# Attention with a gated MLP on one core: where the partial products of the query projection are read, in which order VectorE folds, and when two token quarters are gated

## The chip, the cores and the metric

The kernel runs on one core of one Trainium2 chip. The metric is the device time of one execution in microseconds (us); the number given for a kernel is the median of its runs. A core has several engines with queues of their own: TensorE (PE: matmuls, and PEld: the loading of their weights), VectorE (DVE), ScalarE (ACT), GpSimd (POOL) and SyncE (SP), whose queue issues nearly all DMAs here. Each engine works through its own instructions in order; between engines, semaphores tell when a result is there or a buffer is free. SBUF is the working memory, PSUM the small memory in eight banks that matmuls write into.

## The reference

Sizes: 2048 tokens of width 512, 32 heads of width 128, 2048 cached keys per head, an MLP of width 1792. Inputs are bf16.

```python
xn = layernorm(x)
q = (xn @ wq) split into 32 heads
p = softmax(q @ k_cache.T * 128 ** -0.5)         # per head
s = concat(p @ v_cache) @ wo                     # attention
x1 = xn + shifted(gelu(layernorm(xn) @ w1)) @ w2 # the mixer
g = silu(x1 + gelu(layernorm(x1) @ w3) @ w4)
out = x + s * g
```

## The kernel before, in words

**Head of the program** (about 118 us): layer norms, the mixer and most of the MLP branch, whose result g (up to a factor 0.5) stays in `xall`, one tile of 128 tokens by 512 per token tile t (0 to 15). The rest of the MLP is spread over the first units.

**Units and slots.** The attention is 128 units: `units` lists group g (8 groups of 4 heads), token quarter qt (4 quarters of 512 tokens), head hh in the group, in this order of nesting. A unit has eight slots (`SPU`), n counts slots over all units, u is the unit and p the slot in it. The long loop (L903 on) writes out by hand, slot by slot, in which order every engine gets its instructions; `pin` keeps that order. A slot on TensorE is: two score matmuls (`s_slot`, L405, into one of two PSUM buffers `ps_s`), two value matmuls of ten slots ago (`pv_slot`, L437), then, in some slots, query products and one matmul of the output projection (`wo_mm`, L500; the list `at_wo` gives the slots). ScalarE takes the exponential of the slot's scores, 128x1024 from PSUM to `pT` (L416).

**What VectorE does per unit.** It sums the exponentials over the key blocks, four blocks of 512 at a time: `add_first` (L422, slot 4), `add_next` (L427, slot 6 and slot 0 of the next unit), then folds four blocks to two (`fold`, L431) and two to one (`fold_last`, L435), all in slot 0 of the next unit. In slot 3 SP issues the transposing DMA of that block (`turn`, L460). A unit later, in slot 0 too, `turned_sums` reduces the transposed block (L465), takes the reciprocal (L467) and sends it to DRAM; `bcast` (L473) brings it back, spread over partitions, and `norm` (L485, slot 7) multiplies it into the unit's attention output. `wo_post` (L533) adds a tile's output projection to `sacc` (L549).

**Query projection in pairs.** From unit 14 to 123 the queries of two heads at a time (units v and v+1) come from seven products of half blocks instead of eight (`product`, L363; sums of x and differences of wq are prepared in `x_sum` and `w_sum`, L361). A pair's products 1, 6, 2, 7, 5, 4, 3 are issued at slots 1, 2, 5, 8, 9, 12, 13 counted from the start of unit v-2. They go to one PSUM tile `ps_q` of two halves (256 columns each, together one bank): first M1 in half 0 and M6 in half 1, then M2 is added to half 0; a new tile takes M7 and M5, then M4 is added to half 0 and M3 to half 1. There is one such buffer (psX, tag "xa"), shared in the same order. `q_part` (L383) reads on VectorE what is needed in between:

- part 0, slot 3: a copy m1 = M1 (L388), u = M6 + m1 (L389)
- part 1, slot 6: first quarter of the queries, a copy of M1+M2 (L392)
- part 2, slot 11: u3 = M7 + u (L397), fourth quarter = M5 + u3 (L398)
- part 3, slot 14: the two middle quarters = both halves + u (L400)

So product 2 comes after part 0, product 7 after part 1, product 4 after part 2, and the next pair's product 1 after part 3.

**Gating and output.** For most tiles, in the last group (g = 7) `wo_post` adds the projection to `sacc` (L549), multiplies by the gate (L558), adds x (L560) and sends the tile out (L561). For quarters in `LATE` (before: the last one, tiles 12 to 15) the gate goes in early: after group `GY - 1` (before: 6) `sacc` is multiplied by the gate (`y_scale`, L515) and x is added (`y_add`, L520), in later slots, one tile after the other; from group `GY` on the projection is gated by itself (L542, into `tm`), and either added to `sacc` (L545, if a group follows) or, in the last group, added to it on the way out (`y_out`, L524, when `pay` is called). The last unit and the last quarter's output are written out by hand from L970 on.

Of the kernel before, what the change touches and what calls it, by code (L numbers as in the profile page):

```python
# [8 lines left out]
ACT = mybir.ActivationFunctionType  # L9
ALU = mybir.AluOpType  # L10
FP32 = mybir.dt.float32
BF16 = mybir.dt.bfloat16
# [5 lines left out]
def kernel(  # L18
# [15 lines left out]
    nc = tc.nc  # L34
    P = nc.NUM_PARTITIONS
# [9 lines left out]
    QT = Sq // 512  # L45
# [6 lines left out]
    NG = H // HG  # L52
# [9 lines left out]
    pin = tc.keep_in_program_order  # L62
# [28 lines left out]
    qp2 = ent(pool("qp2", 2))  # L91
    smp = ent(pool("smp", 4))
# [18 lines left out]
    def mm(out, lhsT, rhs, start, stop, **kw):  # L111
# [9 lines left out]
        out=ident[:], in0=diag[:], scalar1=0.0, scalar2=None, op0=ALU.is_equal))  # L121
# [1 line left out]
    HEAD = 7  # L123
    XS = 3 * QT + 1
    units = [(g, qt, hh) for g in range(NG) for qt in range(QT) for hh in range(HG)]
    LATE = (QT - 1,)
    GY = NG - 1
    NU = len(units)
    TURN = range(NU - HG)
    NS = NU * SPU  # L130
    kTs, vBs, wqs, wos, oTs, st = {}, {}, {}, {}, {}, {}
# [202 lines left out]
    sw = {}  # L334
# [28 lines left out]
    def product(v, k):  # L363
# [16 lines left out]
        for dc in range(2):  # L380
            mm(s["ps"][:, side, :], b[:, dc, :], x[:, dc, :], k in (1, 7) and dc == 0, True, skip_group_check=True)

    def q_part(v, i):  # L383
        s = sw[v]
        ps, t = s["ps"], lambda: pS.tile([P, 256], FP32, tag="tq", bufs=3, name="tq")
        if i == 0:
            m1, s["u"] = t(), t()
            pin(nc.vector.tensor_copy(out=m1[:], in_=ps[:, 0, :]))  # L388
            pin(nc.vector.tensor_tensor(out=s["u"][:], in0=ps[:, 1, :], in1=m1[:], op=ALU.add))  # L389
        elif i == 1:  # L390
            q = s["q"] = qp2.tile([P, 4, 256], BF16, name="qT")
            pin(nc.vector.tensor_copy(out=q[:, 0, :], in_=ps[:, 0, :]))  # L392
            for j in range(2):
                st[v + j] = dict(qT=q[:, 2 * j:2 * j + 2, :].rearrange("d a b -> d (a b)"))
        elif i == 2:
            u3 = t()
            pin(nc.vector.tensor_tensor(out=u3[:], in0=ps[:, 0, :], in1=s["u"][:], op=ALU.add))  # L397
            pin(nc.vector.tensor_tensor(out=s["q"][:, 3, :], in0=ps[:, 1, :], in1=u3[:], op=ALU.add))  # L398
        else:
            pin(nc.vector.tensor_tensor(  # L400
                out=s["q"][:, 1:3, :], in0=ps[:], in1=s["u"][:].unsqueeze(1).to_broadcast([P, 2, 256]),
                op=ALU.add))
            del sw[v]
# [21 lines left out]
    def add_next(u, i):  # L425
        a = st[u]["acc"]
        pin(nc.vector.tensor_tensor(out=a[:], in0=a[:], in1=st[u]["pT"][i][:], op=ALU.add))  # L427
# [5 lines left out]
    def fold_last(u):  # L433
        a = st[u]["acc"]
        pin(nc.vector.tensor_tensor(out=a[:, 0, :], in0=a[:, 0, :], in1=a[:, 1, :], op=ALU.add))  # L435
# [25 lines left out]

    def turned_sums(u):
        s = st[u]
        sm = smp.tile([P, 4], FP32, name="sm")
        pin(nc.vector.tensor_reduce(out=sm[:], in_=s["tT"][:], axis=mybir.AxisListType.X, op=ALU.add))  # L465
        rc = smp.tile([P, 4], FP32, name="rc")
        pin(nc.vector.reciprocal(out=rc[:], in_=sm[:]))  # L467
        s["dr"] = drp.tile([P, 4], FP32, name="dr")
        pin(nc.sync.dma_start(out=s["dr"][:], in_=rc[:]))
# [190 lines left out]
    for jc in range(DC):  # L660
        b = BASE_J[jc]
# [200 lines left out]
    UA, UB = NU - 2, NU - 1  # L862
# [12 lines left out]
    pairs = range(FIRST, LAST + 1, 2)  # L875
    q_plan = defaultdict(list)
    steps = defaultdict(list)
    for v in pairs:
        a = (v - 2) * SPU
        for k, n in ((1, 1), (6, 2), (2, 5), (7, 8), (5, 9), (4, 12), (3, 13)):  # L880
            steps[a + n].append((product, v, k))
        for i, n in enumerate((3, 6, 11, 14)):
            steps[a + n].append((q_part, v, i))

    def run_steps(n, which):
        for fn, v, k in steps.get(n, ()):
            if fn is which:
                fn(v, k)
# [4 lines left out]
    for h in range(HG, H, 2):  # L893
        u = (h // HG) * QT * HG + (-4, -2)[h % HG // 2]
# [8 lines left out]
    for n in range(UB * SPU):  # L903
        u, p = divmod(n, SPU)
        extra = len(wo_todo) > 1 and u in (2 * HG, 2 * HG + 1)
        if p == 0 and wo_box:
            wo_slot(4, n, each=1)
        s_slot(u, p)
        pv_run(n)
        for v, dcs in q_plan.get(n, ()):  # L910
            q_mm(v, dcs)
        run_steps(n, product)
        if p == 0 and u - 2 in TURN:
            turned_sums(u - 2)
        if p == 1 and u - 2 in TURN:
            bcast(u - 2)
        if p == 0 and 1 <= u:
            add_next(u - 1, 3)
            fold(u - 1)
            if u != UA:  # L920
                fold_last(u - 1)
        if p == 3 and u - 1 in TURN:
            turn(u - 1)
        if p == 0:
            twice = extra
        if twice and p < 3:
            wo_slot(p, n, tag="xa")
        for v, k in ((u + 1, 3), (u + 2, 7)):
            if p == k and "psq" in st.get(v, ()) and (k == 3) == (v > FIRST):
                q_copy(v)  # L930
        if p == 3:
            run_steps(n, q_part)
        if u - 2 in TURN:
            norm_p, sum_p, wo_p, each = 7, 5, 3, 1
        else:
            norm_p, sum_p, wo_p, each = 4, 5, 4, 1
        at_wo = [wo_p + i for i in range(HG // each + 1)]
        if FIRST - 2 <= u < LAST:
            at_wo = ([0, 3, 4, 6, 7], [0, 2, 3, 6, 7], [3, 4, 5, 6, 7], [0, 2, 3, 6, 7])[u % 4]
        if p == norm_p and 2 <= u and not u - 2 in TURN:  # L940
            norm_queue(u - 2)
        if p == sum_p and 1 <= u and u - 1 not in TURN:
            sums(u - 1)
        if p == sum_p + 1 and 1 <= u and u - 1 not in TURN:
# [9 lines left out]
        if p != 3:  # L954
            run_steps(n, q_part)
# [14 lines left out]
    n = UB * SPU  # L970
    t0 = 4 * (QT - 1)
    ps, tb, yl, whole = {}, {}, {}, {}
# [25 lines left out]
    def pv_to(k):  # L998
# [29 lines left out]
        out=diag[:], in0=diag[:], scalar1=0.0, scalar2=None, op0=ALU.is_equal))  # L1028
# [98 lines left out]
```

## Time and profile before

| | |
|---|---|
| time, median of 3 runs | 1245.12 us (1244.3 to 1245.15) |
| time of the profiled execution | 1244.64 us |
| its span, first to last instruction | 1242.8 us |
| granted TensorE clock | 1.000 |
| units 0, 16, 64, 112, 124 start at | 118.2, 264.5, 674.7, 1084.8, 1194.5 us |
| from the end of unit 123 to the end | 48.3 us |

The profile names an instruction by engine, line, operation and tile (out<-in). "Idle before, releaser" is time in which the engine stood still ahead of an instruction, and what ended it. Matmuls are pipelined: a 512-column matmul is drawn 0.38 us long, while the next one starts 0.22 us after it. Starts are therefore the better measure of TensorE's pace, and of VectorE's and ScalarE's too, whose neighbouring instructions also overlap a little.

### The profile page before, as it was taken

To read this page: it belongs to the slowest core of one execution; us is meant where nothing else is said; L and a number is where in the kernel's file an instruction comes from. 1 tells how busy PE (TensorE), PEld (TensorE's weight loads), DVE (VectorE), ACT (ScalarE), POOL (GpSimd) and SP (SyncE) were. 2 spreads that over 40 slices of the span, in tenths; PEclk is the share of its full clock that TensorE was granted. 3 is DMA by queue.
4 is the path that set the end of the run, shared out by engine and by line. 5 is a ranking of instruction groups with operands and counts; after the bars stand their busy time and mean duration, and the time that the engine had idled before them with its cause. 6 is when DMAs were issued, how large, how long until landed. Compare 5 with 4: busy or idle time off the path is not lost.

```text
span 1242.8 us, 17421 instructions
## 1 busy us (share of the span) xinstructions
PE 1230.5 (99%) x6267; PEld 645.0 (52%) x6267; DVE 1081.4 (87%) x1745; ACT 1092.2 (88%) x1127; POOL 26.8 (2%) x75
## 2 busy tenths in 40 slices
PE   9999999999999999999999999999999999999898
PEld 7444444455555555555555555555555555555445
DVE  7712778899999999999999999999999999999997
ACT  6345999899999999999999999999999999999886
POOL 5300000000000000000000000000000000000000
PEclk9999999999999999999999999999999999999999
DMA  7660123554334524443244423453354433563322
GB/s 176 169 138 31 30 39 65 100 97 88 69 73 106 108 47 85 91 111 77 63 96 98 94 60 82 94 117 61 66 103 94 90 69 74 104 114 68 68 73 82
DMA packets 244055, 107.74 MB, mean 87 GB/s; under 512 B 194816, under 2 KB 227712, under 8 KB 243968
## 3 DMA queue, kind: packets, MB, share of 16 engines
q1 hardware_dynamic: 243408, 106.17, 40.9%
q8 instruction: 49, 0.80, 0.3%
q10 hardware_dynamic: 560, 0.46, 0.1%
q14 instruction: 38, 0.31, 0.1%
HBM read 67.50 MB, written 2.36 MB: 56 GB/s over the span
## 4 chain that ended last, share of the span: by engine, by line
PE 86%; DVE 11%; DMA 2%; ACT 1%; issue 1%; SPq 0%; DVEq 0%; ACTq 0%
PE ps_s L112 35%; PE ps_o L112 33%; PE ps_q L112 7%; PE ps_wo L112 7%; DVE acc L427 3%; PE ps_m L112 2%; DVE oT L485 1%; DVE acc L431 1%; DMA rb<-dr 1%; DVE sm L465 1%; ACT pT L416 1%; DVE sacc L549 1%; DVE xall L558 1%; DVE acc L422 1%; DVE acc L435 1%
## 5 line engine op out<-in xcount | busy, mean ns | idle before, releaser
L416 ACT ACTIVATE pT<-ps_s 128x1024 bf16<-128x1024 f32 x1016 | 1019.7, 1024 | 77.0 <-PE ps_s L112 41.6
L112 PE MATMUL ps_s<-qT,kT 128*128 128x512 bf16 (+1 forms) x2064 | 609.1, 377 | 0.0
L112 PE MATMUL ps_o<-pT,vb 128*128 128x512 bf16 x1984 | 589.9, 379 | 0.0
L427 DVE TENSOR_TENSOR acc<-acc,pT 128x2048 bf16<-128x2048 bf16 x254 | 306.9, 1208 | 11.5 <-ACT pT L416 11.2
L112 PEld LDWEIGHTS <-kT 128*128 128x128 bf16 x2064 | 232.9, 113 | 147.3 <-issue 2.1
L112 PEld LDWEIGHTS <-vb 128*128 128x128 bf16 x1984 | 193.9, 98 | 216.9 <-issue 0.3
L112 PE MATMUL ps_wo<-wo_h,oT 128*128 128x512 bf16 x496 | 186.2, 379 | 0.1
L422 DVE TENSOR_TENSOR acc<-pT 128x2048 bf16<-128x2048 bf16 x127 | 154.8, 1219 | 20.4 <-ACT pT L416 20.1
L431 DVE TENSOR_TENSOR acc<-acc 128x1024 bf16<-128x1024 bf16 x127 | 87.9, 692 | 4.3
L485 DVE TENSOR_TENSOR oT<-ps_o,rb 128x512 bf16<-128x512 f32 x127 | 86.7, 683 | 1.8 <-DMA rb<-dr 1.5
L112 PEld LDWEIGHTS <-oT 128*128 128x128 bf16 x528 | 59.1, 112 | 49.5 <-issue 0.6
L465 DVE TENSOR_REDUCE sm<-tT 128x4 f32<-128x512 bf16 x124 | 84.0, 678 | 0.7 <-DMA tT<-acc 0.7
L549 DVE TENSOR_TENSOR sacc<-ps_wo,sacc 128x512 f32<-128x512 f32 x108 | 73.9, 685 | 0.3 <-PE ps_wo L112 0.3
L112 PEld LDWEIGHTS <-wc 128*128 128x128 bf16 x440 | 43.0, 98 | 58.4 <-issue 8.1
L112 PEld LDWEIGHTS <-wq_h 128*128 128x128 bf16 x398 | 38.9, 98 | 47.9 <-issue 1.8
L112 PE MATMUL ps_q<-xnT,wq_h 128*128 128x256 bf16 (+1 forms) x288 | 61.1, 298 | 1.6 <-DVE tq L389 1.3
L400 DVE TENSOR_TENSOR qT<-ps_q,tq 128x512 bf16<-128x512 f32 x55 | 38.1, 692 | 25.4 <-PE ps_q L112 25.1
L435 DVE TENSOR_TENSOR acc<-acc 128x512 bf16<-128x512 bf16 x127 | 54.0, 425 | 4.3
L293 ACT ACTIVATE h2T<-ps_s 128x1024 bf16<-128x1024 f32 x28 | 28.7, 1025 | 25.9 <-PE ps_s L112 25.9
L112 PEld LDWEIGHTS <-w_sb 128*128 128x128 bf16 x368 | 33.7, 98 | 29.5
L112 PE MATMUL ps_s<-xn2T,w_sb 128*128 128x512 bf16 x224 | 48.8, 379 | 0.0
L112 PE MATMUL ps_q<-xs,wc 128*128 128x256 bf16 x246 | 47.0, 273 | 0.0
(99 smaller groups left out, 574.9 us busy)
## 6 DMA issues: line engine op xcount, KB each, us to landing
rb<-dr SPq DMA_DIRECT2D x127, 256.0 KB, 3.9
vb<-in_A_v_cache_dram SPq DMA_DIRECT2D x62, 256.0 KB, 3.0
wq_h<-in_A_wq_dram SPq DMA_DIRECT2D x32, 128.0 KB, 3.1
wo_h<-in_A_wo_dram SPq DMA_DIRECT2D x32, 128.0 KB, 2.9
w_sb<-in_B_w_dram SPq DMA_DIRECT2D x8, 256.0 KB, 5.0
kT<-in_A_k_cache_dram SPq DMA_TRANSPOSE x128, 2.8
xl<-in_A_x_dram SPq DMA_DIRECT2D x16, 128.0 KB, 2.5
dr<-rc SPq DMA_DIRECT2D x127, 2.0 KB, 1.4
```

Source lines behind the costliest of these rows:

```text
L112: pin(nc.tensor.matmul(out=out, lhsT=lhsT, rhs=rhs, start=start, stop=stop, **kw))
L293: pin(nc.scalar.activation(out=h2[c, f][:], in_=ps[:], func=ACT.Gelu_apprx_tanh))
L400: pin(nc.vector.tensor_tensor(out=s["q"][:, 1:3, :], in0=ps[:], in1=s["u"][:].unsqueeze(1).to_broadcast([P, 2, 256]), op=ALU.add))
L416: pin(nc.scalar.activation(out=s["pT"][-1][:, jj:jj + 2, :], in_=sps[:], func=ACT.Exp, scale=SCALE))
L422: pin(nc.vector.tensor_tensor(out=s["acc"][:], in0=s["pT"][0][:], in1=s["pT"][1][:], op=ALU.add))
L427: pin(nc.vector.tensor_tensor(out=a[:], in0=a[:], in1=st[u]["pT"][i][:], op=ALU.add))
L431: pin(nc.vector.tensor_tensor(out=a[:, 0:2, :], in0=a[:, 0:2, :], in1=a[:, 2:4, :], op=ALU.add))
L435: pin(nc.vector.tensor_tensor(out=a[:, 0, :], in0=a[:, 0, :], in1=a[:, 1, :], op=ALU.add))
L465: pin(nc.vector.tensor_reduce(out=sm[:], in_=s["tT"][:], axis=mybir.AxisListType.X, op=ALU.add))
L485: pin(nc.vector.tensor_tensor(out=to, in0=o, in1=rb, op=ALU.mult))
L549: pin(nc.vector.tensor_tensor(out=sa, in0=ps[:], in1=sa, op=ALU.add))
L558: pin(nc.vector.scalar_tensor_tensor(out=gl, in0=sa, scalar=0.5, in1=gl, op0=ALU.mult, op1=ALU.mult))
```

## The change

Three things, all between units 14 and the end:

1. **Two of a pair's seven reads go to ScalarE** (`q_take`): the copy m1 directly behind product 1 (slot 1, behind that slot's exponential), and the first quarter's copy directly behind product 2 (slot 5). VectorE keeps u, u3, the fourth quarter and the two middle ones.
2. **The remaining reads and the folds are put in another order.** In a pair's first unit u is read in slot 2, between `fold` (still slot 0) and `fold_last` (now slot 2). In its second unit the folds stand in slot 1, in the order u3, `fold`, fourth quarter, `fold_last`. The turned sums are split in two functions that are called one behind the other; they still stand ahead of the last addition.
3. **Early gating for two quarters**: `LATE` has quarters 2 and 3, and `GY` is one group lower, so that scaling, x and gate of tiles 8 to 15 come after group 5, groups 6 and 7 add projections that are gated by themselves, and only tiles 0 to 7 are gated in the last group.

```diff
-    LATE = (QT - 1,)
-    GY = NG - 1
+    LATE = (QT - 2, QT - 1)
+    GY = NG - 2
...
+    def q_take(v, i):
+        s = sw[v]
+        if i == 0:
+            s["m1"] = pS.tile([P, 256], FP32, tag="tq", bufs=3, name="tq")
+            out = s["m1"][:]
+        else:
+            q = s["q"] = qp2.tile([P, 4, 256], BF16, name="qT")
+            for j in range(2):
+                st[v + j] = dict(qT=q[:, 2 * j:2 * j + 2, :].rearrange("d a b -> d (a b)"))
+            out = q[:, 0, :]
+        pin(nc.scalar.activation(out=out, in_=s["ps"][:, 0, :], func=ACT.Identity))
+
     def q_part(v, i):
...
         if i == 0:
-            m1, s["u"] = t(), t()
-            pin(nc.vector.tensor_copy(out=m1[:], in_=ps[:, 0, :]))
-            pin(nc.vector.tensor_tensor(out=s["u"][:], in0=ps[:, 1, :], in1=m1[:], op=ALU.add))
+            s["u"] = t()
+            pin(nc.vector.tensor_tensor(out=s["u"][:], in0=ps[:, 1, :], in1=s["m1"][:], op=ALU.add))
         elif i == 1:
-            q = s["q"] = qp2.tile([P, 4, 256], BF16, name="qT")
-            pin(nc.vector.tensor_copy(out=q[:, 0, :], in_=ps[:, 0, :]))
...
+            s["u3"] = t()
+            pin(nc.vector.tensor_tensor(out=s["u3"][:], in0=ps[:, 0, :], in1=s["u"][:], op=ALU.add))
         elif i == 2:
-            u3 = t()
-            pin(nc.vector.tensor_tensor(out=u3[:], in0=ps[:, 0, :], in1=s["u"][:], op=ALU.add))
-            pin(nc.vector.tensor_tensor(out=s["q"][:, 3, :], in0=ps[:, 1, :], in1=u3[:], op=ALU.add))
+            pin(nc.vector.tensor_tensor(out=s["q"][:, 3, :], in0=ps[:, 1, :], in1=s["u3"][:], op=ALU.add))
...
-        for i, n in enumerate((3, 6, 11, 14)):
-            steps[a + n].append((q_part, v, i))
+        for i, n in enumerate((1, 5)):
+            steps[a + n].append((q_take, v, i))
+        steps[a + 14].append((q_part, v, 3))
+        first[v - 2] = v
+        third[v - 1] = (v,)
+
+    def fold_at(u):
+        return 1 if u in third else 0
...
         run_steps(n, product)
-        if p == 0 and u - 2 in TURN:
-            turned_sums(u - 2)
+        run_steps(n, q_take)
+        if p == 0 and 1 <= u:
+            if u - 2 in TURN:
+                turned_sums(u - 2)
+                turned_recip(u - 2)
+            add_next(u - 1, 3)
         if p == 1 and u - 2 in TURN:
             bcast(u - 2)
-        if p == 0 and 1 <= u:
-            add_next(u - 1, 3)
+        if p == fold_at(u) and 1 <= u:
+            for v in third.get(u, ()):
+                q_part(v, 1)
             fold(u - 1)
-            if u != UA:
+            for v in third.get(u, ()):
+                q_part(v, 2)
+            if u != UA and u not in first:
                 fold_last(u - 1)
+        if p == 2 and u in first:
+            q_part(first[u], 0)
+            fold_last(u - 1)
         if p == 3 and u - 1 in TURN:
             turn(u - 1)
```

More of the change, by code (lines that the diff above doesn't have):

```diff
@@ L386, in q_part @@
         if i == 0:
-            m1, s["u"] = t(), t()
-            pin(nc.vector.tensor_copy(out=m1[:], in_=ps[:, 0, :]))
-            pin(nc.vector.tensor_tensor(out=s["u"][:], in0=ps[:, 1, :], in1=m1[:], op=ALU.add))
+            s["u"] = t()
+            pin(nc.vector.tensor_tensor(out=s["u"][:], in0=ps[:, 1, :], in1=s["m1"][:], op=ALU.add))
         elif i == 1:
-            q = s["q"] = qp2.tile([P, 4, 256], BF16, name="qT")
-            pin(nc.vector.tensor_copy(out=q[:, 0, :], in_=ps[:, 0, :]))
-            for j in range(2):
-                st[v + j] = dict(qT=q[:, 2 * j:2 * j + 2, :].rearrange("d a b -> d (a b)"))
+            s["u3"] = t()
+            pin(nc.vector.tensor_tensor(out=s["u3"][:], in0=ps[:, 0, :], in1=s["u"][:], op=ALU.add))
         elif i == 2:
-            u3 = t()
-            pin(nc.vector.tensor_tensor(out=u3[:], in0=ps[:, 0, :], in1=s["u"][:], op=ALU.add))
-            pin(nc.vector.tensor_tensor(out=s["q"][:, 3, :], in0=ps[:, 1, :], in1=u3[:], op=ALU.add))
+            pin(nc.vector.tensor_tensor(out=s["q"][:, 3, :], in0=ps[:, 1, :], in1=s["u3"][:], op=ALU.add))
         else:
@@ L463, in turned_sums, with turned_recip @@
         s = st[u]
-        sm = smp.tile([P, 4], FP32, name="sm")
+        sm = s["sm"] = smp.tile([P, 4], FP32, name="sm")
         pin(nc.vector.tensor_reduce(out=sm[:], in_=s["tT"][:], axis=mybir.AxisListType.X, op=ALU.add))
+    def turned_recip(u):
+        s = st[u]
+        sm = s["sm"]
         rc = smp.tile([P, 4], FP32, name="rc")
@@ L877 @@
     steps = defaultdict(list)
+    first, third = {}, {}
     for v in pairs:
@@ L930 @@
                 q_copy(v)
-        if p == 3:
-            run_steps(n, q_part)
         if u - 2 in TURN:
@@ L953 @@
             norm_queue(u - 2)
-        if p != 3:
-            run_steps(n, q_part)
+        run_steps(n, q_part)
         if p == 4:
```

## The prediction

> **What bounds the kernel now.** I read the page's busy shares first, then stretches of four units (a unit is one head times 512 queries, eight slots), then who TensorE waited for, then single instructions in order of time.
>
> ```profile
> span 1242.8 us, 17421 instructions
> PE 1230.5 (99%) x6267; PEld 645.0 (52%) x6267; DVE 1081.4 (87%) x1745; ACT 1092.2 (88%) x1127; POOL 26.8 (2%) x75
> ```
>
> PE is busy 99% of the span, so a change that removes no matmul can win only what PE waits for. The profiled execution took 1244.64 us, 1.8 beside its span and 0.5 under the median of 1245.12; the sum below is made on its span, and I apply the difference to the median. The stretches are units 108-111, 112-115, 116-119 and 120-123: length, then PE busy (instructions), PEld, DVE, ACT, POOL, clock, DMA.
>
> ```profile
> 1050.62:1084.79 34.17, 34.17 (x174) 18.02 (x172) 32.52 (x57) 32.16 (x33) 0.00 (x0) 1.00 0.52 97
> 1084.79:1119.67 34.88, 34.36 (x173) 18.01 (x172) 32.36 (x52) 32.15 (x33) 0.00 (x0) 1.00 0.63 114
> 1119.67:1155.60 35.93, 34.46 (x173) 18.04 (x172) 34.48 (x56) 32.16 (x33) 0.00 (x0) 1.00 0.29 63
> 1155.60:1194.49 38.89, 34.94 (x174) 18.01 (x173) 37.23 (x61) 32.16 (x33) 0.00 (x0) 1.00 0.36 72
> ```
>
> The same matmuls take 34.17 where PE never idles; the next three stretches are 0.71, 1.76 and 4.72 longer: **7.2 us lost**. What PE waited for, from 1110 to 1195, from 190 to 1110, and from 1195 on:
>
> ```profile
> PE ps_q L112 <- DVE qT L398: 4.5, 4, 1.7
> PE ps_q L112 <- DVE tq L389: 1.3, 2, 0.7
> ...
> PE ps_q L112 <- DVE qT L398: 0.2, 1, 0.2
> ...
> PE ps_sum L112 <- DVE acc L435: 0.5, 1, 0.5
> PE ps_oh L112 <- DVE oT L485: 0.4, 1, 0.4
> PE ps_o L112 <- DVE oT L485: 0.2, 1, 0.2
> ```
>
> So the loss is products (ps_q) held up by VectorE reading the earlier ones too late; the 5.8 us of waits are 7.2 us of time because modelled matmul ends reach into the gaps. In 920 us of steady running the same wait costs 0.2.
>
> **The change, part by part.** *Two reads leave VectorE* (L388, L392: 55 each), and `q_part` and the folds are interleaved. What VectorE has to do between two products shows in its own starts, here in units 122 and 123, where nothing but its own order holds it:
>
> ```profile
> 1184.83 0.69 DVE L549 TENSOR_TENSOR sacc<-ps_wo,sacc 128x512 f32<-128x512 f32 x1
> 1185.55 0.69 DVE L558 SCALAR_TENSOR_TENSOR xall<-sacc,xall 128x512 bf16<-128x512 f32 x1
> 1186.27 0.42 DVE L560 TENSOR_TENSOR xl<-xall,xl 128x512 bf16<-128x512 bf16 x1
> 1186.61 0.68 DVE L485 TENSOR_TENSOR oT<-ps_o,rb 128x512 bf16<-128x512 f32 x1
> 1187.21 0.68 DVE L465 TENSOR_REDUCE sm<-tT 128x4 f32<-128x512 bf16 x1
> 1187.92 0.18 DVE L467 RECIPROCAL rc<-sm 128x4 f32<-128x4 f32 x1
> 1188.02 1.19 DVE L427 TENSOR_TENSOR acc<-acc,pT 128x2048 bf16<-128x2048 bf16 x1
> 1189.25 0.69 DVE L431 TENSOR_TENSOR acc<-acc 128x1024 bf16<-128x1024 bf16 x1
> 1189.97 0.42 DVE L435 TENSOR_TENSOR acc<-acc 128x512 bf16<-128x512 bf16 x1
> 1190.32 0.42 DVE L397 TENSOR_TENSOR tq<-ps_q,tq 128x256 f32<-128x256 f32 x1
> 1190.77 0.42 DVE L398 TENSOR_TENSOR qT<-ps_q,tq 128x256 bf16<-128x256 f32 x1
> ...
> 1192.74 0.69 DVE L400 TENSOR_TENSOR qT<-ps_q,tq 128x512 bf16<-128x512 f32 x1 [0.42 <-PE ps_q L112]
> 1193.35 1.22 DVE L427 TENSOR_TENSOR acc<-acc,pT 128x2048 bf16<-128x2048 bf16 x1
> 1194.48 0.69 DVE L549 TENSOR_TENSOR sacc<-ps_wo,sacc 128x512 f32<-128x512 f32 x1
> ```
>
> Read starts, not durations: an instruction that needs its forerunner's result starts 0.03 after its end (L427 to L431: 1.23 for a 1.19), one that doesn't starts 0.08 before it (L427 to L549: 1.13 for a 1.22). An unrelated read put between addition and fold thus saves 0.11 at each seam. The time that VectorE is given goes from a pair's last read (L400) to the next pair's product 4, which waits for L398; in a quiet place:
>
> ```profile
> 604.66 0.69 DVE L400 TENSOR_TENSOR qT<-ps_q,tq 128x512 bf16<-128x512 f32 x1 [0.53 <-PE ps_q L112]
> 620.23 0.38 PE L112 MATMUL ps_q<-xnT,wc 128*128 128x256 bf16 x2
> ```
>
> **15.57 us.** Before, in the late units, the chain is L400 0.61 and an addition 1.13; a block from L549 to the end of the folds of 0.72+0.72+0.34+0.60+0.71+0.10+1.23+0.72+0.35 = 5.49; an L520 0.60; L388 0.45, L389 0.34, first addition 1.13, L392 0.33, addition 1.13; the block again; an L515 0.60, L397 0.45, L398 0.42: 18.2, over by 2.6, which is the longest wait on L389 and the longest on L398 together (0.7 + 1.7). After, L520, L515, L388 and L392 are gone (2.0), the last fold stands behind product 4's read (0.35), and four seams of 0.11 go (fold to L389; addition, L397, fold, L398): **15.4**, which fits by about 0.2. L389, for product 2, loses L388 and the last fold ahead of it, 0.8, where the longest wait was 0.7.
>
> *Early gating.* Quarter 2 is treated as quarter 3 was, both one group earlier.
>
> ```profile
> L361 DVE TENSOR_TENSOR wc<-wq_h 128x256 bf16<-128x256 bf16 x28 | 8.0, 285 | 0.0
> ```
>
> Per tile, L515 and L520 move from units 115-122 to 95-110 (one per unit, quarter 2 new), tiles 8-15 of group 6 pay a gating (L542) and an addition (L545) in place of L549, 0.7 more in units 111-118, and at the end L558 and L560 become one addition (L524). In 95-118 a unit holds two operations of 0.6 to 0.7 where the late block has 1.78, so the chain is 1 us shorter than 15.4; the four weight differences per pair in 108-111 (L361, 0.2 each with the overlap) leave it under 15.57 too. Eight tiles' loads of x move some 16 units ahead on SP with as many outputs as before. I cost it at 0; the cover is that 0.2 to 1 us. From unit 124 on, one gating of 0.6 stands where L549, L558 and L560 took 1.78 ahead of the folds and of L485: the three waits of the tail, **1.1**, go. With 0.2 from the steady part, the gain is 7.2 + 0.2 + 1.1 = **8.5**.
>
> *What it adds: ScalarE, and a wait of PE on it.* A copy stands behind the exponential of slots 1 and 5 of each pair. What one costs there:
>
> ```profile
> 193.17 1.02 ACT L416 ACTIVATE pT<-ps_s 128x1024 bf16<-128x1024 f32 x1
> 194.08 0.63 ACT L306 ACTIVATE th<-xall 128x512 bf16<-128x512 bf16 x1
> ...
> L623 ACT ACTIVATE tb<-ps_r 128x256 bf16<-128x256 f32 x4 | 1.5, 384 | 1.3 <-PE ps_r L112 1.2
> ```
>
> Another function starts 0.91 after an exponential starts, 0.11 before that ends; 256 columns from PSUM take 0.38. So with the same overlap a copy takes 0.27 of ScalarE, 0.54 per pair of 17.1 us. Exponentials back to back would need 0.91 each, 14.6 per pair: there is room. A slot takes 34.17 / 32 = 1.07, and 0.91 + 0.27 = 1.18: the next exponential is late by 0.11, the one after it no more, and scores have two buffers that cover it.
>
> But a copy and product 6 share a bank, two halves of one tile. Does the product wait for a reader of the other half?
>
> ```profile
> 1151.43 0.42 DVE L397 TENSOR_TENSOR tq<-ps_q,tq 128x256 f32<-128x256 f32 x1
> 1151.88 0.42 DVE L398 TENSOR_TENSOR qT<-ps_q,tq 128x256 bf16<-128x256 f32 x1
> 1152.36 0.38 PE L112 MATMUL ps_q<-xnT,wc 128*128 128x256 bf16 x2 [1.33 <-DVE qT L398]
> ```
>
> Product 4 writes half 0, whose reader L397 had ended at 1151.85; it started 0.06 after L398, the reader of half 1. So the bank is kept as one, and product 6 will wait for the copy issued one slot before. The Trainium skill, "PSUM — Partial Sum Buffer", section "PSUM bank collisions raise a hardware error", has the same rule (guard by bank, not by address) and so speaks against this change; were it by address, the sum would be 5.0 better, the first rival. The price, in units 84 and 86, which stand for the two patterns of even units:
>
> ```profile
> 847.29 1.02 ACT L416 ACTIVATE pT<-ps_s 128x1024 bf16<-128x1024 f32 x1
> 848.60 0.38 PE L112 MATMUL ps_q<-xs,wc 128*128 128x256 bf16 x2
> ...
> 864.24 1.03 ACT L416 ACTIVATE pT<-ps_s 128x1024 bf16<-128x1024 f32 x1
> 865.45 0.38 PE L112 MATMUL ps_q<-xs,wc 128*128 128x256 bf16 x2
> ```
>
> Copy start 0.91 after the exponential, 0.38 long, 0.06 to PE: product 6 could start at 848.64 and 865.59, 0.04 and 0.14 late. Behind it stand all of PE's matmuls, so each is a loss: 27 x 0.04 + 28 x 0.14 = **5.0 us**. No row shows PE waiting for ScalarE, hence bounds: 0 if it doesn't wait; and if the copy starts only when the exponential has ended and takes the 0.42 that VectorE's copy L388 takes, 0.19 and 0.30, 13.5 in all. I take 5.0, by the rows that show ScalarE itself. The skill's "ScalarE: Activation LUTs", section "What ACT_TABLE_LOAD costs", gives 0.19 us and 0.83 ns per column, with 0.09 of overlap: by that estimate a copy ends 0.04 later, and the time would be 2 us more. The second copy, in slot 5, has three slots until product 7 takes the bank: 0.
>
> Sum: 5.0 - 8.5 = -3.5, so 1241.1 for the profiled execution and **1241.6** for the median.
>
> **The rivals.** *No wait on the bank*: product 6 runs beside the copy. Against it: the six waits from 1110 on are all put down to the second reader (L398, L389). It gives 1245.1 - 8.5 = 1236.6.
>
> *Slower: the copies pace PE.* With copies at the upper bound, product 6 is late by 0.25 on average, 13.5 in 55 pairs, against 8.5: 1250.1. It decides from a mean wait of 8.5 / 55 = 0.155 on, against 0.09 computed. For it: ScalarE's 32.16 busy of 34.17 in units 108-111; against it: the 0.11 overlap in the rows of L306.
>
> *The turned sums come late.* The last fold now comes 0.2 (first unit) to 0.35 us later, and the transposing DMA of L460 with it.
>
> ```profile
> DMA to landing us min/median/max: 3.4/3.7/5.8
> ```
>
> That is tT from issue to landing. In the late chain the fold ends some 5.2 us before the next L465 needs it (the rest of 0.35, then 1.13+0.61+1.13+0.72+0.72+0.34+0.60); longer landings stall VectorE, where only 0.2 is spare. At some 0.35 in each of units 116-123 that is 2.8: 1244.4.
>
> **How the numbers follow.** Forecast 0.52 (own range 1238.5 to 1244, by a hop or copy of 0.05 either way), no bank wait 0.12, late sums or another part of the gain lost 0.14, copies that pace PE 0.22. A measurement of this kernel can tell about 0.2% (2.5 us) from no change. Faster than 1242.6: 0.8 of the forecast, the first rival, little of the third: 0.56. Slower than 1247.6: most of the fourth, 0.20. The rest, 0.24, lies between. The range 1236.4 to 1249.0 takes in the first rival's point and leaves out half of the slower case.
>
> **What would show it.** Right: units 120-123 last 34.2 to 34.6 instead of 38.89; units 108-111 last about 34.35 instead of 34.17, with product 6 waiting for ScalarE in each pair, 0.04 and 0.14 in turn; ScalarE's new copies at 0.38; no wait on L398's successor. Wrong: steady units unchanged (no bank wait), or longer by over 0.3 per pair (copies pace PE); waits of ps_q on VectorE left in 115-123 (the moved work or the late transpose); waits of VectorE on tT.

## The result, and the profile after

The kernel after takes **1240.68 us** (median of 7 runs, 1240.19 to 1241.13) against 1244.72 (7 runs, 1243.95 to 1245.29) for the kernel before, run beside it: ratio **0.9968 [0.9956, 0.9979]**, faster by 0.3%, which lies just above what can be told from no change. The prediction was 1241.6. The profiled execution took 1240.9 us with a span of 1239.1.

Lines have moved. ScalarE's copies are L393, the exponential L423; on VectorE u is L400, u3 L403, the fourth quarter L405, the middle quarters L407, the additions L429 and L434, the folds L438 and L442, the turned sum L472, `norm` L496, `y_scale` L526, the addition to `sacc` L560.

The page's first lines of after: VectorE works 51 us less, ScalarE 20 us more, and PE is drawn busy all the time.

```profile
span 1239.1 us, 17537 instructions
PE 1233.0 (100%) x6267; PEld 644.2 (52%) x6267; DVE 1030.3 (83%) x1647; ACT 1112.6 (90%) x1237; POOL 26.7 (2%) x75
```

What PE waited for from 240 us on in after, the whole list:

```profile
PE ps_q L112 <- DVE qT L405: 0.6, 2, 0.4
PE ps_o L112 <- DVE oT L496: 0.2, 1, 0.2
```

The waits of 1.7 and 1.3 that the prediction started from are gone. PE's waits on ScalarE, forecast at 5 us, are not in this list, because the modelled end of the matmul ahead covers them: in unit 86 that matmul is drawn to 867.85, and product 6, which waits, starts at 867.83. They have to be read from starts and lengths. Stretches of after, units 108-111, 112-115, 116-119 and 120-123 (columns as in the prediction):

```profile
1054.12:1088.99 34.87, 34.47 (x174) 17.99 (x173) 32.80 (x57) 32.91 (x37) 0.00 (x0) 1.00 0.50 99
1088.99:1123.37 34.38, 34.38 (x173) 18.04 (x172) 31.96 (x52) 32.90 (x37) 0.00 (x0) 1.00 0.55 111
1123.37:1157.68 34.31, 34.31 (x174) 18.05 (x172) 32.09 (x51) 32.91 (x37) 0.00 (x0) 1.00 0.30 62
1157.68:1192.10 34.42, 34.42 (x173) 18.00 (x172) 33.36 (x54) 32.91 (x37) 0.00 (x0) 1.00 0.35 77
```

Units 120-123 went from 38.89 to 34.42, where 34.2 to 34.6 was forecast. Units 108-111 went from 34.17 to 34.87, where 34.35 was forecast; unit 109 alone is 0.52 longer than before. To see where the 3.7 us of span came from, the run is cut in four, at the first exponential of units 14, 94, 112 and 124 (some 0.7 behind the first score matmul of a unit, at which the stretches above are cut): units 14-93, 94-111, 112-123, and 124 to the end. First before, then after:

```profile
247.53:931.65 684.12, 683.77 (x3442) 360.48 (x3441) 639.19 (x1013) 643.17 (x641) 0.00 (x0) 1.00 0.41 86
931.65:1085.48 153.83, 153.83 (x776) 81.12 (x775) 143.39 (x229) 144.64 (x146) 0.00 (x0) 1.00 0.43 85
1085.48:1195.18 109.70, 103.76 (x518) 54.05 (x517) 104.06 (x164) 96.48 (x98) 0.00 (x0) 1.00 0.42 83
1195.18:1242.78 47.60, 43.05 (x289) 25.87 (x287) 39.00 (x70) 36.04 (x45) 0.00 (x0) 1.00 0.28 78
```

```profile
247.34:934.20 686.86, 686.85 (x3442) 360.34 (x3441) 596.69 (x933) 657.85 (x722) 0.00 (x0) 1.00 0.41 85
934.20:1089.68 155.48, 154.84 (x776) 81.09 (x775) 143.27 (x228) 148.10 (x164) 0.00 (x0) 1.00 0.47 91
1089.68:1192.79 103.11, 103.11 (x518) 54.08 (x517) 97.41 (x151) 98.71 (x110) 0.00 (x0) 1.00 0.40 84
1192.79:1239.13 46.34, 42.70 (x289) 25.99 (x287) 37.11 (x66) 36.01 (x45) 0.00 (x0) 1.00 0.27 69
```

So +2.74, +1.65, -6.59, -1.26 (and -0.2 ahead of unit 14): the long steady part pays, the end gains. The payment per pair is seen in ScalarE's and PE's starts of unit 84, after (a row of the timeline: start, duration, engine, line, operation):

```profile
849.49 1.02 ACT L423 ACTIVATE pT<-ps_s 128x1024 bf16<-128x1024 f32 x1
850.41 0.38 ACT L393 ACTIVATE tq<-ps_q 128x256 f32<-128x256 f32 x1
850.84 0.38 PE L112 MATMUL ps_q<-xs,wc 128*128 128x256 bf16 x2
```

The copy starts 0.92 after the exponential and ends at 850.79; product 6 starts 0.05 later. In unit 86 the same rows are 866.48, 867.38 (0.40 long) and 867.83. From one unit's first exponential to the next, units like 84 take 8.46 instead of 8.425, units like 86 take 8.57, and odd units 8.64 as before: 0.03 and 0.14 more, in turn. Quiet units agree to 0.01 between the traces of one kernel (8.46 and 8.57 again in after_again, below), so such differences can be read from single executions.

### The profile page after: what moved, and what is told of

The parts are those of the page before. It is cut to its first block, busy times and chain, and to the rows that moved or that the text cites. A ratio compares the mean times of both kernels' runs of the same rounds, so it can differ in the third digit from the quotient of the medians.

```text
span 1239.1 us, 17537 instructions
## 1 busy us (share of the span) xinstructions
PE 1233.0 (100%) x6267; PEld 644.2 (52%) x6267; DVE 1030.3 (83%) x1647; ACT 1112.6 (90%) x1237; POOL 26.7 (2%) x75
## 4 chain that ended last, share of the span: by engine, by line
PE 95%; DVE 3%; DMA 1%; ACT 1%; issue 0%; POOL 0%; DVEq 0%; ACTq 0%
PE ps_s L112 39%; PE ps_o L112 37%; PE ps_q L112 8%; PE ps_wo L112 8%; PE ps_m L112 2%; DVE acc L434 1%; ACT pT L423 1%; DMA rb<-dr 0%; DMA tT<-acc 0%; DVE sm L472 0%; DVE oT L496 0%; DMA xin<-in_A_x_dram 0%; PE ps_oh L112 0%; DMA dr<-rc 0%; DVE y L1014 0%
## 5 line engine op out<-in xcount | busy, mean ns | idle before, releaser
L423 ACT ACTIVATE pT<-ps_s 128x1024 bf16<-128x1024 f32 x1016 | 1019.8, 1025 | 54.4 <-PE ps_s L112 24.8
L434 DVE TENSOR_TENSOR acc<-acc,pT 128x2048 bf16<-128x2048 bf16 x254 | 307.0, 1209 | 54.6 <-ACT pT L423 54.1
L429 DVE TENSOR_TENSOR acc<-pT 128x2048 bf16<-128x2048 bf16 x127 | 155.4, 1224 | 43.0 <-ACT pT L423 41.9
L438 DVE TENSOR_TENSOR acc<-acc 128x1024 bf16<-128x1024 bf16 x127 | 87.4, 688 | 2.5
L496 DVE TENSOR_TENSOR oT<-ps_o,rb 128x512 bf16<-128x512 f32 x127 | 86.6, 682 | 1.5 <-DMA rb<-dr 1.2
L472 DVE TENSOR_REDUCE sm<-tT 128x4 f32<-128x512 bf16 x124 | 83.9, 677 | 2.0 <-DMA tT<-acc 2.0
L560 DVE TENSOR_TENSOR sacc<-ps_wo,sacc 128x512 f32<-128x512 f32 x96 | 65.7, 684 | 0.0
L407 DVE TENSOR_TENSOR qT<-ps_q,tq 128x512 bf16<-128x512 f32 x55 | 38.0, 692 | 23.7 <-PE ps_q L112 23.5
L442 DVE TENSOR_TENSOR acc<-acc 128x512 bf16<-128x512 bf16 x127 | 53.0, 417 | 0.5
```

The costliest lines, as they stand in the source:

```text
L407: pin(nc.vector.tensor_tensor(out=s["q"][:, 1:3, :], in0=ps[:], in1=s["u"][:].unsqueeze(1).to_broadcast([P, 2, 256]), op=ALU.add))
L423: pin(nc.scalar.activation(out=s["pT"][-1][:, jj:jj + 2, :], in_=sps[:], func=ACT.Exp, scale=SCALE))
L429: pin(nc.vector.tensor_tensor(out=s["acc"][:], in0=s["pT"][0][:], in1=s["pT"][1][:], op=ALU.add))
L438: pin(nc.vector.tensor_tensor(out=a[:, 0:2, :], in0=a[:, 0:2, :], in1=a[:, 2:4, :], op=ALU.add))
L496: pin(nc.vector.tensor_tensor(out=to, in0=o, in1=rb, op=ALU.mult))
L560: pin(nc.vector.tensor_tensor(out=sa, in0=ps[:], in1=sa, op=ALU.add))
```

## The experiments

**Theory.** Three things make up the result. Product 6 waits for ScalarE's copy, because both touch one PSUM tile, which is one bank (5 us lost). The shorter order on VectorE lets products come in time in the late units (7 us won). In units 97 and 109 a DMA came late and the operations that early gating moved there left VectorE no room (1 us lost). **Rivals:** the steady units are longer because ScalarE has more to do, not because of the bank; the late gain comes from early gating, not from the reads and their order; the leftovers, or the whole difference, belong to single executions.

The kernel before ran beside each of the three sets (medians 1246.95, 1247.63, 1247.48), and each ratio is against that one. The sets ran on three chips (7, 13 and 4); which chip the first comparison ran on, with 1244.72 for before, is not on record. All its 7 runs of before lie under all 46 of the three sets (at most 1245.29, at least 1245.77), so times of different sets are compared with care below.

### What lengthens the steady units

**p6_slot3**: product 6 and u one slot later, all else as after.

```diff
-        for k, n in ((1, 1), (6, 2), (2, 5), (7, 8), (5, 9), (4, 12), (3, 13)):
+        for k, n in ((1, 1), (6, 3), (2, 5), (7, 8), (5, 9), (4, 12), (3, 13)):
...
-        if p == 2 and u in first:
+        if p == 3 and u in first:
```

> Product 6 and the read u one slot later (slot 3 for slot 2), all else as in the changed kernel. Theory (the bank makes product 6 wait for ScalarE's copy of m1, which ends 0.03 or 0.14 us after the product's place): a slot later the copy has long ended, units 84 and 86 are back at 8.43 us from 8.46 and 8.57, 55 pairs give back 27 x 0.03 + 28 x 0.14 = 4.7 us, about 1236.0. Rival (it is ScalarE's added load, 0.54 us per pair, that slows TensorE through the scores' two buffers): the copies are all still there, so about 1240.7 as the changed kernel.

Measured: 1237.65 us (1236.96 to 1238.75), ratio 0.9922 [0.9909, 0.9934]. Units 14-93, and what PE waited for from 240 us on, in p6_slot3:

```profile
247.25:930.60 683.35, 683.35 (x3442) 360.49 (x3441) 597.24 (x933) 654.23 (x722) 0.00 (x0) 1.00 0.43 86
```

```profile
PE ps_q L112 <- DVE qT L405: 1.9, 4, 0.8
```

With the same copies on ScalarE, even units are back at 8.43: 3.5 us less than after over 40 pairs, 0.09 for each, which is the price of the wait. The second view shows the other side: PE now runs up to VectorE's chain more often (1.9 drawn instead of 0.6; units 97, 103, 107, 109, 115 and 121 are longer than in a quiet place). So the span falls by 2.7 us and not by the 4.7 expected.

**m1_twice** and **m1_sbuf** do the copy m1 a second time on ScalarE. In the first the second copy reads the bank again, in the second it reads and rewrites the SBUF tile; the values are the same. Each kernel has one of the two added lines; the labels behind them are mine.

```diff
         pin(nc.scalar.activation(out=out, in_=s["ps"][:, 0, :], func=ACT.Identity))
+        if i == 0:
+            pin(nc.scalar.activation(out=out, in_=s["ps"][:, 0, :], func=ACT.Identity))  # m1_twice
+            pin(nc.scalar.activation(out=out, in_=out, func=ACT.Identity))               # m1_sbuf
```

> The copy of m1 made twice on ScalarE, both from PSUM; product 6 in slot 2. Theory: product 6 now waits for the second copy, which ends one copy's share of ScalarE (0.27 us) later, in every pair: 55 x 0.27 = 14.9 us more than the changed kernel, about 1255.5, units 84 and 86 at 8.73 and 8.84. Rival (ScalarE's load): ScalarE has room for 0.27 more per 17.1 us (16 x 0.91 + 3 x 0.27 = 15.4), so under 3 us more.

> A second ScalarE pass of the same width behind the copy of m1, but reading and writing m1 in SBUF, so that it loads ScalarE and holds no PSUM bank. Theory: product 6 waits for the first copy alone, nothing else gets later: 1240.7 as the changed kernel, within 1 us. Rival (ScalarE's load is what costs): as much as with the copy made twice from PSUM, 3 to 15 us more.

Measured: m1_twice 1263.52 us (1262.95 to 1263.85), ratio 1.0128 [1.0114, 1.0142]; m1_sbuf 1245.37 (1244.36 to 1246.34), ratio 0.9985 [0.9976, 0.9995]. Unit 84 of m1_twice, and the longest item of PE's waiting from 240 us on (ScalarE's second copy is L395, the exponential L425):

```profile
864.67 0.38 ACT L393 ACTIVATE tq<-ps_q 128x256 f32<-128x256 f32 x1
865.08 0.38 ACT L395 ACTIVATE tq<-ps_q 128x256 f32<-128x256 f32 x1
865.52 0.38 PE L112 MATMUL ps_q<-xs,wc 128*128 128x256 bf16 x2 [0.29 <-ACT tq L395]
```

```profile
PE ps_q L112 <- ACT tq L395: 18.7, 55, 0.4
```

Here the wait is long enough to be drawn, once in each of the 55 pairs, with ScalarE as its releaser. Product 6 writes half 1 of the bank and the copy reads half 0, so the program's waits keep the tile, here one bank, as one; whether the chip would bear the two at once wasn't tried. A second copy costs 0.41 per pair (unit 84 takes 8.87, unit 86 takes 8.98) against the 0.27 expected: it writes the tile of the first and starts 0.03 after that ends, where two unrelated instructions overlap by 0.11. Unit 84 of m1_sbuf:

```profile
853.26 0.38 ACT L393 ACTIVATE tq<-ps_q 128x256 f32<-128x256 f32 x1
853.67 0.42 ACT L395 ACTIVATE tq<-tq 128x256 f32<-128x256 f32 x1
853.99 2.83 ACT L425 ACTIVATE pT<-ps_s 128x1024 bf16<-128x1024 f32 x3
...
853.69 0.38 PE L112 MATMUL ps_q<-xs,wc 128*128 128x256 bf16 x2
```

Product 6 starts 0.05 after the first copy's end (853.64), beside the second copy, so it is the bank that it waits for and not ScalarE's queue. But the kernel was expected to be equal to after, and it isn't: its span is 1244.5 against 1239.1, inside the 3 to 15 us of the rival, with units 14-93 3.0 us longer, 0.07 per pair. m1_twice, with the same number of copies, is 22.9 us longer than after. The next exponential starts 0.73 after the first copy, in after 0.27 (850.68 in unit 84); the PSUM buffer that it reads comes free 0.46 later, and the scores that take it start at 855.05, 0.05 after that exponential's end (853.99 and 1.00). The rival is thus true beyond a limit: two score buffers cover the one copy of the change, as p6_slot3 shows, and not two.

**m1_vector**: m1 on VectorE again, ahead of u; the second copy stays on ScalarE.

```diff
-            s["u"] = t()
+            s["m1"], s["u"] = t(), t()
+            pin(nc.vector.tensor_copy(out=s["m1"][:], in_=ps[:, 0, :]))
...
-        for i, n in enumerate((1, 5)):
-            steps[a + n].append((q_take, v, i))
+        steps[a + 5].append((q_take, v, 1))
```

> One read of seven on ScalarE: the copy of m1 goes back to VectorE, between the fold and u in slot 2, where product 6 has been issued already; the second copy stays on ScalarE. Theory: no wait of product 6 on a reader, 4.7 us back; VectorE's chain from one pair's last read to the next pair's product 4 is 0.45 longer, 15.9 against 15.57 in the two last pairs only and in units with late DMAs, 0.3 to 0.5 each, 1 to 1.5 us in all: about 1237. Rival (VectorE's relief from both reads is needed all along): the waits of ps_q on VectorE come back in units 95 to 123 and the time is that of the changed kernel, 1240 or more.

Measured: 1239.57 us (1238.89 to 1241.52), ratio 0.9939 [0.9926, 0.9951]. PE's longest item of waiting from 240 us on in m1_vector:

```profile
PE ps_q L112 <- DVE qT L406: 2.4, 6, 0.8
```

L406 is the read that product 4 waits for. Even units are 8.43 here too, the third run that agrees with the bank wait; VectorE's chain is longer instead, and the waits on it are 2.4 instead of 0.6; so the time lies 2.6 above the 1237 expected, just under the rival's 1240. With its span of 1237.8 the kernel stands 1.3 under after, so where product 6 stands, moving m1 to ScalarE seems to cost a little more than it brings; executions of one kernel differ by more, so that isn't settled. p6_slot3, with m1 on ScalarE and product 6 a slot later, is 1.9 faster than this one.

### What shortens the late units

**reads_only** (after, with the gating of before; its edit is shown) and **gating_only** (before, with the gating of after; the same edit reversed):

```diff
-    LATE = (QT - 2, QT - 1)
-    GY = NG - 2
+    LATE = (QT - 1,)
+    GY = NG - 1
```

> The changed kernel with the gating of before (last quarter, last group), so copies on ScalarE and the new order alone. Theory: the wait of product 6 costs 4.7 as in the changed kernel; the chain with L526 and L531 back in the late pairs is 16.6 in units 120 and 121 and 16.0 in 122 and 123, over by 1.0 and 0.4; the tail keeps its 1.2 of waits: 1 us under before, ratio 0.9985 to 1.0. Rival (the reads' relief alone is enough): the changed kernel's time, ratio 0.997.

> The kernel before with early gating for two quarters and group 6, and nothing else of the change. Theory (VectorE's chain between a pair's last read and the next pair's product 4, allowed 15.57 us, decides): without L515 and L520 the chain of the two last pairs is 17.0, over by 1.4 each; with two more operations per pair it is 16.1 in units 111 to 118 (three pairs, 0.5 each) and 15.8 to 16.6 in 95 to 110 (eight pairs, 0.2 to 1.0); 8 to 9 us of waits where before had 7.2, less 1.2 in the tail: within 1.5 us of before on either side, ratio 0.999 to 1.001. Rival (the late gating alone caused the waits): the whole gain of about 8.5 us and no wait on ScalarE, ratio 0.993.

Measured: reads_only 1243.6 us (1243.37 to 1244.26), ratio 0.9969 [0.9957, 0.998]; gating_only 1249.81 (1248.53 to 1251.83), ratio 1.0018 [1.001, 1.0027]. Units 94-111, 112-123 and the end in reads_only; then the longest item of PE's waiting in gating_only from 940 us on, that is from unit 94:

```profile
934.20:1088.74 154.54, 153.66 (x760) 81.00 (x775) 134.03 (x211) 148.10 (x163) 0.00 (x0) 1.00 0.47 86
1088.74:1193.97 105.23, 102.98 (x508) 54.04 (x517) 97.94 (x152) 98.73 (x110) 0.00 (x0) 1.00 0.47 86
1193.97:1241.58 47.61, 42.85 (x285) 25.87 (x287) 38.99 (x70) 36.04 (x45) 0.00 (x0) 0.98 0.30 79
```

```profile
PE ps_q L112 <- DVE qT L398: 9.3, 11, 1.4
```

The reads and the order alone take 4.5 of the 6.6 us out of units 112-123 (109.70 to 105.23). How they share the 4.5, the reads or the order, was not tried. Gating adds the other 2.1 (1.2 against after_again, whose units 112-123 take 104.00) and 1.27 at the end, and costs 0.94 in 94-111. On before's order hardly more than the end wins (46.32 long; units 112-123 take 109.06): eleven waits of up to 1.4 stand between units 95 and 123, units 94-111 take 160.28, and the time goes up by 2.2, a little more than the 1.5 expected. So the second rival falls; early gating pays only on a chain that has room. By its ratio, which is after's own, reads_only would bear out its rival instead; but before ran slower beside it. Against after its span is 1241.6 to 1239.1, and to 1240.9 in after_again. What tells them apart in both is the place: the end is 47.61 long against 46.34 and 46.33, and units 119 and 123 are 0.5 longer.

**no_gating_late**: all_later (below) with the gating of before.

> Product 6 in slot 3; scaling, addition of x and the last group's gating later (as in the kernel with all of them later), but early gating as before, for the last quarter in the last group alone. Theory: with L526 and L571 behind product 4's read the late pairs' chain is 14.9 against 15.57 and needs no early gating; what is lost is the tail's 1.3 us of waits, so 1.3 us over the kernel with early gating, about 1237.0. Rival (early gating is needed for the late units): waits of 2 us and more come back in 117 to 123, 1239 or more.

Measured: 1239.9 us (1239.17 to 1240.1), ratio 0.9935 [0.9922, 0.9947], 3.8 above y_later, which was run again beside it. Its span is 3.5 longer: units 94-111 are as in y_later, 112-123 are 0.5 longer (104.31 against 103.80), and the end is 49.40 long against 46.34. PE's waits from 240 us on in no_gating_late (L560 is the addition to `sacc`):

```profile
PE ps_wo L112 <- DVE sacc L560: 1.7, 3, 0.7
PE ps_oh L112 <- DVE oT L496: 1.4, 1, 1.4
PE ps_sum L112 <- DVE acc L442: 0.7, 1, 0.7
```

Of these, 1.2 for `ps_wo` stand in units 120 and 123, the rest behind. More was lost than expected, though in the place that was expected: early gating is worth about 3 us here after unit 123, where, as in before, the gating of the last tiles stands ahead of the last folds. Part of that is this kernel's own. It also moves the last gating five slots on, and ahead of the `norm` (L496) that `ps_oh` waits for 1.4 us, VectorE waits 1.05 for a late load of x. reads_only, which has neither, loses 1.27 there.

### What is left, and what belongs to single executions

**y_later**: p6_slot3, and the two moved operations of early gating four slots later, behind the reads that products wait for. **all_later** moves the last group's gating by five slots too.

```diff
-            at(k, lambda: y_scale(t))
-            at(k + SPU, lambda: y_add(t))
+            at(k + 4, lambda: y_scale(t))
+            at(k + SPU + 4, lambda: y_add(t))
```

> Product 6 in slot 3, and the scaling and the addition of x (L526, L531) four slots later, so behind product 4's read in a pair's second unit and in a stretch where VectorE waits for product 3 anyway. Theory: the waits left in units 97, 103, 107 and 109 (0.61, 0.19, 0.36, 0.99 with product 6 in slot 3) lose 0.6 each at most, 1.5 to 1.8 us in all under the kernel with product 6 in slot 3 alone, ratio to before about 0.991. Rival (the late DMAs in those units hold VectorE whatever stands behind them): as with product 6 in slot 3 alone, 0.992.

> As the kernel before this one in the list, and in the last group the gating and the addition of x (L569, L571) five slots later too, so behind product 4's read of the next unit. Theory: the waits of units 115 and 121 (0.26, 0.77) go as well, another 0.8 to 1.0 us; ratio to before about 0.990. Rival: the operations only move into the end of the kernel and delay it by as much: as the kernel before this one in the list.

Measured: y_later 1235.7 us (1235.55 to 1236.87), ratio 0.9908 [0.9893, 0.9923]; all_later 1235.91 (1235.74 to 1236.35), ratio 0.9908 [0.9895, 0.9922]. Unit 97 shows why, first VectorE and PE in after, then the same in y_later (in brackets the idle time before, and its releaser):

```profile
948.97 0.69 DVE L407 TENSOR_TENSOR qT<-ps_q,tq 128x512 bf16<-128x512 f32 x1 [0.37 <-PE ps_q L112]
...
957.91 1.23 DVE L434 TENSOR_TENSOR acc<-acc,pT 128x2048 bf16<-128x2048 bf16 x1 [0.67 <-ACT pT L423]
...
961.12 0.69 DVE L472 TENSOR_REDUCE sm<-tT 128x4 f32<-128x512 bf16 x1 [0.78 <-DMA tT<-acc]
...
961.93 1.20 DVE L434 TENSOR_TENSOR acc<-acc,pT 128x2048 bf16<-128x2048 bf16 x1
963.04 0.68 DVE L526 SCALAR_TENSOR_TENSOR sacc<-sacc,xall 128x512 f32<-128x512 f32 x1
963.64 0.42 DVE L403 TENSOR_TENSOR tq<-ps_q,tq 128x256 f32<-128x256 f32 x1
963.98 0.68 DVE L438 TENSOR_TENSOR acc<-acc 128x1024 bf16<-128x1024 bf16 x1
964.58 0.42 DVE L405 TENSOR_TENSOR qT<-ps_q,tq 128x256 bf16<-128x256 f32 x1
...
965.05 0.38 PE L112 MATMUL ps_q<-xnT,wc 128*128 128x256 bf16 x2 [0.24 <-DVE qT L405]
```

```profile
957.59 0.69 DVE L472 TENSOR_REDUCE sm<-tT 128x4 f32<-128x512 bf16 x1 [0.87 <-DMA tT<-acc]
...
958.41 1.19 DVE L434 TENSOR_TENSOR acc<-acc,pT 128x2048 bf16<-128x2048 bf16 x1
959.52 0.42 DVE L403 TENSOR_TENSOR tq<-ps_q,tq 128x256 f32<-128x256 f32 x1
959.85 0.68 DVE L438 TENSOR_TENSOR acc<-acc 128x1024 bf16<-128x1024 bf16 x1
960.45 0.42 DVE L405 TENSOR_TENSOR qT<-ps_q,tq 128x256 bf16<-128x256 f32 x1
...
961.03 0.38 PE L112 MATMUL ps_q<-xnT,wc 128*128 128x256 bf16 x2
```

The turned block comes late in both, in y_later even by 0.87 instead of 0.78. But in after `y_scale` (L526) stands between the late sum and L405, the read that product 4 waits for; in y_later it has gone behind it, and product 4 starts on time, 0.16 after that read's end. VectorE's waits for tT were 4.7 us in y_later and 2.0 in after, yet no wait for ps_q is left in y_later. Both a late DMA and the moved work were needed: in reads_only, where nothing was moved there, the block of unit 97 came late by 1.00, and PE did not wait. all_later brought nothing more: the waits that it should have removed, in units 115 and 121, weren't in that execution of y_later. They are in a second one (0.4 and 0.8), so whether it would help there stays open.

**before_again**, **after_again** and **y_later_again** are the three kernels unchanged, to see how much of a difference belongs to an execution (and, as said, to another chip).

> The kernel before, unchanged, for its trace: it was timed at 1244.7 beside the changed kernel but at 1247.0 and 1247.6 beside the experiments. The trace of early gating alone has 2.6 us more than the first trace of before in units 14 to 94, where the two kernels are the same. Theory: the kernel before has no spare time on VectorE in units 14 to 31 (sums of x), so that slower transposes and broadcasts there turn into waits of product 4; where the time is near 1247, units 14 to 94 last over 686 us instead of 684.1 and show waits of ps_q on VectorE there. Rival: the difference lies in the head or is spread evenly over all units.

> The changed kernel, unchanged, beside the same runs of before. Theory: with VectorE's reads gone it has that spare time, so it takes 1240.7 within 0.5 whatever before takes; the ratio to before is 0.9968 where before takes 1244.7 and 0.995 where it takes 1247. Rival: everything is slower by the same share, 1243 where before takes 1247, ratio 0.9968.

> Product 6 in slot 3 and scaling and addition of x four slots later, unchanged, beside the changed kernel. Theory: 4.7 us from the bank, about 0.9 from the waits of units 97 and 109: 5.5 us under the changed kernel, 1235.5 within 0.7. Rival: it was only as fast as it was beside a slower before; then less than 3 us under the changed kernel.

Measured: 1247.26 us (1245.87 to 1249.7), ratio 1.0 [0.9991, 1.001]; 1241.68 (1241.13 to 1242.67), ratio 0.9951 [0.9938, 0.9963]; 1236.14 (1235.66 to 1236.63), ratio 0.9906 [0.9892, 0.9919]. Here tT took this long from issue to landing in before_again, and these are the longest items of PE's waiting there from 240 us on:

```profile
DMA to landing us min/median/max: 3.5/4.2/6.5
```

```profile
PE ps_q L112 <- DVE qT L398: 6.8, 10, 1.7
PE ps_q L112 <- DVE tq L389: 1.7, 3, 0.7
```

The median landing is 4.2 where the first trace of before had 3.7, VectorE waited 4.2 us for tT instead of 0.7, and before loses 3.3 us more in units 14-111 (686.02 and 155.24), with waits of ps_q in units 14 to 29, as expected, and in 61, 97 and 109; its late units are unchanged (109.50). After, with 3.9 here and 3.6 in its first trace, has the same steady part (686.85) and is 1.7 longer from unit 94 to 123, in units 97, 107, 109, 115 and 121; its median lies above what was expected. So executions differ where DMAs come late, and before, whose chain has no room, is longer by more; that may be why the ratio is 0.9951 here and was 0.9968, though the intervals overlap. Whether the later landings belong to the execution or to the chip, these traces don't separate. The third rival is true for 1 to 3 us, not for the difference itself.

**y_later beats both kernels**: 1236.14 against 1241.68 for after and 1247.26 for before in the same set.

## Why the prediction was right

The terms, as the prediction put them, beside what the traces show:

| term | forecast, us | measured, us | from |
|---|---|---|---|
| product 6 waits for the copy | +5.0 | +4.7 | 27 x 0.03 + 28 x 0.14, by even units |
| late units 112-123 | -7.2 | -7.1 | -6.59 and the 0.5 of six copies in it |
| end of the run | -1.1 | -1.3 | 47.60 to 46.34 |
| steady waits of before | -0.2 | -0.8 | 0.59 and 0.24 in units 15 and 17, gone |
| early gating's cover | 0 | +0.9 | units 94-111, 154.54 in reads_only to 155.48 |

The measured column sums to -3.6; the span shows -3.7. Units 16 and 73 are 0.20 and 0.16 longer than before (0.16 each in p6_slot3, too); I haven't followed them up.

**The bank wait** came where it was forecast, for both patterns of units, though no row of before showed PE waiting for ScalarE. What carried it was the row of product 4 behind the second reader, and for the size three rows: another function starts 0.91 after an exponential (0.92 and 0.90 measured), 256 columns take 0.38 (0.38 and 0.40), and a hop to PE takes 0.06 (0.05). The Trainium skill's rule to guard by bank, "PSUM — Partial Sum Buffer", section "PSUM bank collisions raise a hardware error", is kept by this program, as m1_twice shows, where ScalarE reads the other half. The Trainium skill's "ScalarE: Activation LUTs", section "What ACT_TABLE_LOAD costs", gives 0.19 us and 0.83 ns per column, by which a copy would take an estimated 0.40; the groups have these (busy, mean ns of one):

```profile
L393 ACT ACTIVATE tq<-ps_q 128x256 f32<-128x256 f32 x55 | 21.5, 391 | 0.0
L393 ACT ACTIVATE qT<-ps_q 128x256 bf16<-128x256 f32 x55 | 20.8, 377 | 0.0
```

The estimate is nearly right for the first; the 2 us that it gave on top of the rows didn't come.

**The late chain** was the step with the least room: 15.4 against 15.57. Here it is in after, up to unit 121: the pair's last read, the second addition, and the read that product 4 waits for.

```profile
1155.94 0.69 DVE L407 TENSOR_TENSOR qT<-ps_q,tq 128x512 bf16<-128x512 f32 x1 [0.19 <-PE ps_q L112]
...
1164.80 1.23 DVE L434 TENSOR_TENSOR acc<-acc,pT 128x2048 bf16<-128x2048 bf16 x1 [0.21 <-ACT pT L423]
...
1171.18 0.42 DVE L405 TENSOR_TENSOR qT<-ps_q,tq 128x256 bf16<-128x256 f32 x1
```

From the first start to the last end it takes 15.66, of which VectorE waits 0.21 for an exponential and works 15.45; before, the same chain takes 18.19, where 18.2 was computed. (The 2.6 over is only loosely the drawn 0.7 + 1.7; by lengths, units 120 and 121 of before are 0.76 and 1.93 too long.) The room was so small that after shows 0.11 of extra time in unit 121 beyond the copies' waits, after_again 0.76, where the DMAs came later. What it says of the cause is shown by reads_only and gating_only: the order and the reads carry 4.5 of the 6.6.

**The mis-sized term** is "I cost it at 0; the cover is that 0.2 to 1 us". In the chain that ends in unit 97 VectorE's own work is 14.58, 1.0 under 15.57, near what was computed. But the prediction let the second addition start when VectorE is free, and there it waits 0.67 for ScalarE's exponential (the row of L434 at 957.91, above). That leaves a cover of 0.3 against a turned block that is 0.78 late; the chain takes 16.03 and the unit is 0.40 too long. In the chain that ends in unit 109 the same wait is 0.59, and the chain takes 16.11. The third rival named the mechanism (a late turned block with only 0.2 spare) but put it in units 116-123; it struck in 97 and, with a late reciprocal spread (rb) that the prediction didn't name, in 109. Waits of VectorE on tT were one of the prediction's own signs of being wrong; they came, and with that of rb they cost 1 us. The steady gain, which was put too small by 0.6, made up for most of it, and that was luck. Nothing of the fourth case appeared: copies at the upper bound would have made even units 0.19 and 0.30 longer.

## What to carry to other kernels

When a read is moved to another engine, ask what the next writer of that bank waits for: here a copy of 0.38 us on another engine held the next product by 0.09 on average, and one slot more between them gave that back. Count an engine's work between two fixed points of the schedule, start to start, rather than its busy share, and keep work that has no deadline behind the reads that have one. A chain with 0.2 us to spare turns late DMAs into waits, so compare such kernels in several executions before giving a small difference a cause. And count in such a chain what its own instructions wait for: here a wait of 0.6 for an exponential took most of the room that was counted for early gating.

## What the runs showed of the hardware that was not expected

- Two instructions of ScalarE that depend on each other start 0.03 us after one another's end (m1_twice, m1_sbuf), where unrelated ones overlap by 0.11: a second 0.38 us copy costs 0.41 rather than 0.27.
- The same transposing DMAs of the same kernel landed in a median of 3.7 us in one execution and 4.2 in another (in another set, perhaps on another chip), and with that the kernel before took some 3 us more.
- A wait of PE of 0.03 to 0.14 us does not appear as a wait in the profile, and one that makes unit 84 of m1_twice 0.45 longer than before is drawn as 0.29: short waits must be read from the lengths of units.
